# A fused window attention and expert mixture: one scaling step on ScalarE, an earlier landing time in the planner, and a new order of the work

## The chip, the cores and the metric

The kernel runs on 1 core of one Trainium2 chip. The metric is the device time of one execution in microseconds, as the median of the runs. The core's engines are TensorE (matmuls, PE in the profile; PEld is its weight load), VectorE (DVE), ScalarE (ACT), GpSimd (POOL) and SyncE (SP). Each has its own queue of instructions and works through it in order; PSUM has eight banks, and matmuls write there.

## The reference

Inputs are q, k, v of shape (4, 8, 768, 64), gate probabilities of shape (3072, 4), w1 of shape (4, 512, 1024) and w2 of shape (4, 1024, 512).

```python
scores = (q @ k.T) / sqrt(64)
keep = (pos_k < 4) | ((0 <= pos_q - pos_k) & (pos_q - pos_k < 128))
a = softmax(where(keep, scores, -1e9))
x = (a @ v).transpose(0, 2, 1, 3).reshape(3072, 512)
p = domain_probs / (domain_probs.sum(-1) + 1e-9)
out = sum over e of p[:, e] * (relu(x @ w1[e]) @ w2[e])
```

Attention sees a window of 128 keys and four sink keys; the mixture runs all four experts for every token.

## The kernel before, in words

**Tiles and groups.** Each of the four batches b has 768 tokens, cut into three groups g of 256; a pair (b, g) is the unit in which tokens pass from attention to the experts. Attention works on head pairs hp. For each (b, hp, g) it makes scores (L708, for the sinks L669), an exponential on ScalarE (L733), a mask product on VectorE (L727, L742), values (L767, L774), a reciprocal (L801) and a scaling (L804, L819). The result is turned into xT, with TensorE (L838) in batch 0 and with a transposing DMA (L791) after that.

**Experts.** Groups (0, 0) and (0, 1) are the *early* groups. For them the hidden rows H = relu(x w1) are made ungated. `emit_second` then multiplies by w2 in eight 512-column matmuls (L1579) for each half group s and expert e, into one of two `acc` banks. VectorE adds the result, scaled by the gate column, to `osbw`: L1589 writes the first (e = 0), L1591 adds the others. All other groups multiply the gate into H, sum all experts in PSUM, and use a scheme with seven block products in place of eight for the second matmul (L1493, names P1 to P7, in the order of CHAIN). VectorE prepares weight forms for it (L360 to L366) and sums of H blocks, S (L1434, L1411).

The first matmul also has a seven-product way (START says from which group for each expert), with its weight forms (L393 to L399) and token forms T (L1174): L1208 with 128 columns, or L1320 with 512 columns for the *turned units*. These last are the units of batches 2 and 3 but for the first four. They write H rows by token (L1341, L1345 and others), and a transposing DMA from SP (L1301) turns these into H. Units that don't take that way use L1118. A unit of the seven-product way takes two PSUM banks X and Y from a ring of six at P1, and one, V, at P5.

**What sets the order.** The Python program is a planner that writes a fixed order for each engine. It keeps a clock for each (`t`, with the costs in `pe`, `act`, `dve`, `pool`, `lands` and `sp`) and at every turn it lists what could go next on TensorE with a ready time and a priority (the lower number goes first): an attention step (DUE when it is due, 3 otherwise), a step of an open unit (2, plus STEP0 for each place in the list), a newly opened unit (OPEN when one is open already), a second product (1, or LOW_SECOND), or a block product (HIGH_PRODUCT when VectorE is BEHIND or many H tiles are live, LOW_PRODUCT otherwise). Attention is due by SHARE_OF, and a batch's attention begins by LEAD. OVER says by how many steps attention must be late before a single head pair's scores go without a partner. MIX bounds the early units left when later ones may open, FULL and NH (6) the live H tiles.

Work for VectorE and ScalarE goes into a list by `later(engine, ready, slack, run)`, and `flush` takes from it, of what is ready, what has the earliest `ready + slack`. The slacks are named: MASK for the mask product, GATE and GATE0 for the gated evictions, TOKEN for T, FORM for the weight forms, SCALED for ScalarE's second step on a turned row. MARGIN goes into the due time of S sums, and CHORES bounds how many of them stand in the list. SOON is the time from which weight forms are made. All these only set the order in the queues; semaphores do the real waiting.

**H rows.** In `emit_turning`, the DMA's time to land is counted by the same clock, and S sums and products of a unit are offered from then on:

```python
done = sp(at, issue=1330, takes=1400, turning=True) + LANDS
self.H_part[b, g, e](done)
```

where `sp` adds the issue, 800 ns, `takes` and 900 ns. EXPERTS gives the order of the four experts of a pair (all in order where it names none).

Of the kernel before, what the change touches and what calls it, by code (L numbers as in the profile page):

```python
# [9 lines left out]
ALU = mybir.AluOpType  # L10
# [6 lines left out]
def kernel(  # L17
# [12 lines left out]
    nc = tc.nc  # L30
# [5 lines left out]
    Ntok, Dout = out.shape  # L36
# [24 lines left out]
    TURN_ABOUT = 1  # L61
    OWN = 2
    TURNED_UNITS = (4, 0)
    EXPERTS = {(1, 0): (0, 2, 1, 3), (1, 1): (3, 2, 1, 0), (1, 2): (3, 2, 1, 0), (2, 2): (2, 0, 3, 1), (3, 1): (3, 2, 1, 0)}
    FIRST = 1
    START = {0: (1, 0), 1: (0, 2), 2: (0, 0), 3: (1, 0)}
    MIX = 6
    SHARE_OF = (1.01, 0.92, 0.96)
    LEAD = (1.01, 0.99)
    DUE = 1.9  # L70
    LOW_PRODUCT = 2.9
    LOW_SECOND = 2.7
    HIGH_PRODUCT = 1.9
    EARLY = -0.01
    MASK = 5000
    GATE = 800
    GATE0 = 300
    FORM = 6000
    TOKEN = 3000
    MARGIN = 500  # L80
    HOLD = 0
    FULL = 7
    STEP0 = 0.03
    READY = 40
    REST = 3000
    LANDS = 0
    SCALED = 300
    SHARED = 2
    MARGIN1, MARGIN2 = 4000, 14000
    OWNED_READ = 152  # L90
    WIDE = 2
    OPEN = 2.5
    SOON = 34000
    NEARLY = 2
    ROWED = 24000
    GATED = 38000
# [5 lines left out]
    MORE = 2  # L102
    BOTH = 1
    PAIR = 0
    OVER = 4
    ALONE = 2.0
    BEHIND = 1500
    CHORES = 3
    BIASED = 1
    FAST = tuple(START)  # L110
    BZ = 0
# [17 lines left out]
    def act(cols, *deps):  # L129
        at = max([t["act"], *deps])  # L130
        t["act"] = at + max(196, 68 + cols / 1.23)
        return at + max(350, 205 + cols / 1.2)
# [29 lines left out]
    def later(engine, ready, slack, run):  # L162

        pend.append((ready, ready + slack, engine, run))
# [255 lines left out]
    def next_form():  # L420
# [11 lines left out]
        forming.append(x)  # L432
        later("dve", t["pe"], FORM, run)
        return True
# [58 lines left out]
    for h in range(H):  # L493
        r = 32 * (h // 2) + NSINK * (h % 2)
        nc.sync.dma_start(
            out=vsf[r:r + NSINK, :, 0:D], in_=v[:, h, 0:NSINK, :].rearrange("b j d -> j b d"),
# [4 lines left out]
    for sgn in (1, -1):  # L501
        nc.gpsimd.affine_select(
            out=identf, in_=identf, compare_op=ALU.is_ge, fill=0.0,
# [6 lines left out]
    for tb in (2, 3):  # L510
# [21 lines left out]
        out=low[0].rearrange("p (n q) -> p n q", n=3)[:, 0::2], in0=two, scalar1=LOW, scalar2=-LOW, op0=ALU.mult, op1=ALU.add,  # L532
# [4 lines left out]
        out=sel2, in_=ident.rearrange("p (n c) -> p n c", c=32)[:, :, 0:2 * NSINK].rearrange("p n (a j) -> p n a j", a=2), axis=AX.X,  # L537
# [151 lines left out]
    def scores(b, hp, g, more=False):  # L689
# [34 lines left out]
        else:  # L724
            def mask_both(at):
                def run(engine):
                    nc.vector.tensor_mul(a, a, m[:, None, :].to_broadcast([P, 2, w]))  # L727
                    masked(dve(2 * w, rate=1.92))
                later("dve", at, MASK, run)
            part = join(2, mask_both)  # L730
# [226 lines left out]
    acc_free = [0.0, 0.0]  # L957
    out_sb = {}

    class Mixture:  # L960


        def __init__(self):
# [3 lines left out]
            for b, g in PAIRS:  # L967
                fast = [e for e in EXPERTS.get((b, g), range(E)) if self.is_fast(b, g, e)]
                slow = [e for e in range(E) if e not in fast]
# [40 lines left out]
        def halves(self):  # L1010
            return sum(x[0] <= t["pe"] + REST for x in self.resting)

# [52 lines left out]
        def firsts(self):  # L1065
# [4 lines left out]
            for i, u in enumerate(self.open):  # L1070
                b, g, e = u["unit"]
                if u["fast"]:
                    for m in u["left"]:
                        yield max(u["at"].get(m, 1e12), free_at() if m == "P5" else 0.0), 2 + STEP0 * i, (u, m)
                else:
                    j = u["left"][0]
                    yield self.unit_ready(b, g, e, j), 2 + STEP0 * i, (u, j)
            if n < WIDE and early:
                at, g = self.next_early()
                yield at, (OPEN if n else 2), ("early", g)  # L1080
            if n < WIDE and self.units and (self.units[0][0] or loaded) and early <= MIX and self.room() and not (early + zero and self.live >= NH - 1):
                yield self.unit_ready(*self.units[0], QF), (OPEN if n else 2) - EARLY, ("unit",)

        def emit_first(self, what, ready):
# [56 lines left out]
            def run(engine):  # L1141
# [5 lines left out]
                part(at)  # L1147
            later("dve", end, GATE0, run)

        def tokens(self):  # L1150
# [22 lines left out]
            def run(engine):  # L1173
# [4 lines left out]
                else:  # L1178
                    self.T_at[b, g] = done
            later("dve", at, TOKEN, run)  # L1180

        def emit_fast(self, u, m, ready):
# [67 lines left out]
            if m == "P1":  # L1250
                u["last"] = join(2, lambda at: gated(H[:, 1, :, 1], tiles["X"], 1, at, GATE, slots["X"]))

# [19 lines left out]
            elif m == "P2":  # L1272
                gated(H[:, 0, :, 1], y, 1, end, GATE, slots["Y"])
            elif m == "P7":
# [5 lines left out]
            elif m == "P3":  # L1280
                gated(H[:, 0, :, 0], y, 0, end, GATE, slots["V"])
            else:
                u["last"](end)

        def emit_turning(self, u, m, ready):
# [4 lines left out]
            if m in ("P1", "P5"):  # L1290
                spare = [i for i in range(6) if ring[i] <= ready + 40]
                spare.sort(key=lambda i: (whole[i], ring[i]))
                if m == "P1":
# [5 lines left out]
                    def turned(k):  # L1299
                        def turn(at):  # L1300
                            nc.sync.dma_start(  # L1301
                                out=H[:, k].rearrange("c f t n -> c (f t) n"), in_=X[k].rearrange("p f t n -> p (f t n)"), transpose=True,
                            )
                            done = sp(at, issue=1330, takes=1400, turning=True) + LANDS
                            self.H_part[b, g, e](done)
# [27 lines left out]
            def gated(k, s, src, ready, slack, slot=None, then=None):  # L1333
                gate = own_gates[:, 2 * ((b - OWN) * NG + g) + s, e:e + 1]

                def run(engine):
                    if engine == "act":
                        nc.scalar.activation(out=src, in_=src, func=AF.Relu)  # L1338

                        def scaled(engine):  # L1340
                            nc.scalar.mul(X[k][:, :, s], src, gate)  # L1341
                            done(act(n))
                        later("act", act(n), SCALED, scaled)
                        return
# [11 lines left out]
            if m == "P1":  # L1356
                u["last"] = join(2, lambda at: gated(1, 1, tiles["X"], at, GATE, slots["X"]))

# [19 lines left out]
            elif m == "P2":  # L1378
                gated(0, 1, y, end, GATE, slots["Y"])
            elif m == "P7":  # L1380
# [5 lines left out]
            elif m == "P3":  # L1386
                gated(0, 0, y, end, GATE, slots["V"])
            else:
# [54 lines left out]
        def until(self, b, g, e, m):  # L1443
            n = self.products.index((b, g, m)) * E + self.order_of(b, g).index(e) - self.piece
            return max(0.0, n * QF * G / 2.4 - MARGIN)

# [119 lines left out]
        def emit_second(self):  # L1566
            ready = self.second_ready()
            g, s, e = self.second.pop(0)
            if g not in out_sb:
                out_sb[g] = mo.tile([P, 2, Dout], FP32, name="osbw", tag=f"wide{g}", bufs=1)  # L1570
                if g == 0:
                    gates()
            dst = out_sb[g][:, s]
            bank = self.turn % 2
            self.turn += 1
            op = acc[bank]
            H = self.H[0, g, e]
            for fb in range(NFB):
                nc.tensor.matmul(  # L1579
                    op, lhsT=H[:, fb // QF, fb % QF, s], rhs=w2_sb[e][:, fb, :],  # L1580
                    start=(fb == 0), stop=(fb == NFB - 1),
                )
            end = pe(NFB * Dout, ready, n=NFB)
            acc_free[bank] = 1e12
            sc = scale_t[:, 2 * g + s, e:e + 1]

            def run(engine):
                if e == 0:
                    nc.vector.tensor_scalar(out=dst, in0=op, scalar1=sc, scalar2=None, op0=ALU.mult)  # L1589
                else:  # L1590
                    nc.vector.scalar_tensor_tensor(  # L1591
                        out=dst, in0=op, scalar=sc, in1=dst, op0=ALU.mult, op1=ALU.add,
                    )
                acc_free[bank] = at = dve(Dout, fixed=218)
                if e == E - 1:
                    r = (2 * g + s) * P
                    nc.sync.dma_start(out=out[r:r + P, :], in_=dst)
                    self.stored.append(sp(at))
            later("dve", end, 400, run)
            self.since = 0  # L1600
            self.done += NFB * Dout
            if s == 1:
                self.live -= 1
                left[e] -= 1
                if not left[e]:
                    used.add(e)
# [55 lines left out]
    while mix.more() or att.more():  # L1662
# [46 lines left out]
        mix.chore()  # L1709
        if ahead or now > SOON:  # L1710
            next_form()
        if ahead + 1 < B and not att.more() and (ahead == 0 or (ahead + 1, 0) in turned_at) and (ahead == 0 or mix.done >= sum(work[:ahead]) * LEAD[ahead - 1]):
            ahead += 1
# [5 lines left out]
            upto = mix.done  # L1719
        share = (sum(work[:ahead]) - upto) * SHARE_OF[max(ahead - 1, 0)]  # L1720
        due = ahead == 0 or att.steps * share <= (mix.done - upto) * att.total
        opts = []
        if att.more():
            late = ahead == 0 or (att.steps + OVER) * share <= (mix.done - upto) * att.total
            for r, step in att.options():
                p = (DUE if due else 3) - 0.1 * (step == "two")
                if step == "one" and not late:
                    p = max(p, DUE + ALONE)
                opts.append((max(r, now), p, "att", step))
        s2, p = mix.second_ready(), mix.product_ready()  # L1730
        behind = max(t["dve"] - now, 0.0) + 500 * sum(x[2] == "dve" and x[0] < now + 300 for x in pend)
        opts.append((max(p, now), HIGH_PRODUCT if behind > BEHIND or mix.live >= FULL or wide and TURN_ABOUT and mix.turn_about else LOW_PRODUCT, "product", None))
        joins = due and ahead >= PAIR and att.two() and not late and len(mix.open) >= HOLDS
        opts += [(max(f, now), p, "first", x) for f, p, x in mix.firsts() if not (joins and x[0] in ("unit", "early"))]
        opts.append((max(s2, now), 1 if mix.since >= 1 else LOW_SECOND, "second", None))
        soonest = min(o[0] for o in opts)
# [61 lines left out]
```

## Time and profile before

| | us |
|---|---|
| median of 3 runs (353.9 to 354.16) | 354.09 |
| span of the profiled execution | 351.9 |
| TensorE busy | 346.2 |
| VectorE busy | 282.8 |
| ScalarE busy | 208.3 |
| GpSimd busy | 71.6 |

The profiled execution's own time is given by its span, from the first to the last instruction; the device time of the runs is 2.2 us longer than that, which lies around the span. The granted TensorE clock is 1.000 over the span. TensorE's busy time counts matmuls that overlap and whose ends are modelled, so it is read together with the starts of the matmuls. In the windows view a line has the window, its length, and for PE, PEld, DVE, ACT and POOL the busy us and the number of instructions, then the granted clock, the DMA engines' use and GB/s. In a line of the timeline the first two columns are start and duration; what stands in brackets is idle time of the engine and what ended it.

### The profile page before, as it was taken

The numbers are of one execution on the slowest core, as the hardware profiler recorded it, in microseconds if no ns is written. First come the engines' busy times: TensorE is split into PE (matmuls) and PEld (weight loads), VectorE is DVE, ScalarE is ACT, GpSimd is POOL, SyncE is SP. The second block draws the span as 40 slices with busy tenths as digits, with TensorE's granted clock in tenths as the row PEclk, the third lists the DMA queues.
The fourth block names the chain that finished last, engine by engine and source line by source line (L and its number), as shares of the span: only waits on it lengthen the run. The fifth ranks groups of instructions, "written<-read, shape, count | busy, mean of one in ns | idle before, by whom it ended". The sixth has DMA issues, their size and how long they took to land.

```text
span 351.9 us, 9351 instructions
## 1 busy us (share of the span) xinstructions
PE 346.2 (98%) x3721; PEld 266.0 (76%) x3721; DVE 282.8 (80%) x672; ACT 208.3 (59%) x476; POOL 71.6 (20%) x89
## 2 busy tenths in 40 slices
PE   8999999999999999999999999999999999999996
PEld 3685769656789998998999886755856676666685
DVE  5886999878999999799898999578768586675740
ACT  6863624447874443647453539689589767666611
POOL 8946114330546206100152000000000000000000
PEclk9999999999999999999999999999999999999999
DMA  9999999999999999920999602545437733545441
GB/s 178 178 188 195 223 214 181 179 160 174 162 147 165 121 145 122 132 64 9 109 173 159 113 32 62 120 101 120 80 91 174 127 89 93 120 120 115 67 120 61
DMA packets 161032, 45.61 MB, mean 130 GB/s; under 512 B 144740, under 2 KB 156996, under 8 KB 160988
## 3 DMA queue, kind: packets, MB, share of 16 engines
q0 software_dynamic: 79104, 17.31, 56.4%
q1 hardware_dynamic: 80828, 27.18, 40.1%
q8 instruction: 29, 0.48, 0.5%
q10 hardware_dynamic: 1056, 0.52, 0.5%
q14 instruction: 15, 0.12, 0.1%
HBM read 38.39 MB, written 6.34 MB: 127 GB/s over the span
## 4 chain that ended last, share of the span: by engine, by line
PE 75%; DMA 19%; POOL 5%; issue 1%; ACT 0%; POOLq 0%; SPq 0%
PE acc L1493 35%; PE cps L1320 17%; PE cps L1208 15%; DMA w<-in_moe_w_dram 12%; DMA qkn<-in_k_dram 4%; DMA qkT<-qkn 3%; PE sps L708 3%; PE od L774 2%; POOL qkn L251 2%; POOL w L331 1%; POOL vx L318 1%; PE hps L1118 1%; PE od L767 1%; POOL w L341 0%; PE acc L1579 0%
## 5 line engine op out<-in xcount | busy, mean ns | idle before, releaser
L1493 PEld LDWEIGHTS <-H 128*128 128x128 bf16 x708 | 66.5, 98 | 17.9 <-issue 1.1
L1493 PE MATMUL acc<-w,H 128*128 128x256 bf16 x420 | 56.9, 273 | 0.0
L733 ACT ACTIVATE aT<-sps 128x512 bf16<-128x512 f32 (+1 forms) x96 | 47.2, 579 | 16.3 <-PE sps L708 16.2
L1208 PEld LDWEIGHTS <-w 128*128 128x128 bf16 x640 | 39.1, 98 | 1.2 <-issue 0.5
L1493 PEld LDWEIGHTS <-S 128*128 128x128 bf16 x320 | 30.3, 98 | 9.5 <-issue 0.8
L1241 DVE SCALAR_TENSOR_TENSOR H<-cps,gates 128x512 bf16<-128x512 f32 x54 | 36.6, 683 | 0.0
L1338 ACT ACTIVATE cps<-cps 128x512 f32<-128x512 f32 x44 | 25.5, 585 | 17.5 <-PE cps L1320 17.0
L1118 PE MATMUL hps<-xT,w 128*128 128x256 bf16 x256 | 31.9, 273 | 0.1
L819 ACT ACTIVATE onat<-od,R 128x64 bf16<-128x64 f32 x108 | 24.9, 324 | 11.4 <-DVE R L801 11.1
L318 POOL DMA_DIRECT2D vx<-in_v_dram x24 | 21.4, 903 | 43.0 <-PE od L774 31.2
L1208 PEld LDWEIGHTS <-vf 128*128 128x128 bf16 x480 | 29.3, 98 | 1.0 <-issue 0.5
L1579 PE MATMUL acc<-w,H 128*128 128x512 bf16 x128 | 29.9, 379 | 0.0
L1493 PE MATMUL acc<-wf,H 128*128 128x256 bf16 (+1 forms) x216 | 29.6, 272 | 0.0
L1118 PEld LDWEIGHTS <-w 128*128 128x128 bf16 x256 | 24.1, 98 | 4.7 <-issue 0.9
L1341 ACT ACTIVATE rest<-cps,own_gates 128x512 bf16<-128x512 f32 x37 | 25.5, 693 | 0.7
L727 DVE TENSOR_TENSOR aT<-aT,mask 128x1024 bf16<-128x1024 bf16 (+1 forms) x36 | 22.7, 640 | 3.1 <-ACT aT L733 2.8
L251 POOL DMA_DIRECT2D qkn<-in_q_dram x22 | 19.7, 896 | 23.3 <-DMA qkT<-qkn 14.7
L1208 PE MATMUL cps<-T,w 128*128 128x128 bf16 x320 | 24.3, 219 | 0.0
L1208 PE MATMUL cps<-xT,w 128*128 128x128 bf16 x320 | 24.1, 219 | 0.0
L1320 PE MATMUL cps<-w,T 128*128 128x512 bf16 x80 | 23.8, 379 | 0.0
L1320 PE MATMUL cps<-vf,T 128*128 128x512 bf16 x80 | 23.6, 379 | 0.0
L1554 ACT COPY osb<-acc 128x256 f32<-128x256 f32 x32 | 12.1, 382 | 19.3 <-PE acc L1493 19.1
(145 smaller groups left out, 673.5 us busy)
## 6 DMA issues: line engine op xcount, KB each, us to landing
w<-in_moe_w_dram POOLq DMA_DIRECT2D x6, 1024.0 KB, 18.4
out_dram<-osb SPq DMA_DIRECT2D x16, 256.0 KB
vx<-in_v_dram POOLq DMA_DIRECT2D x24, 128.0 KB, 6.5
qkn<-in_q_dram POOLq DMA_DIRECT2D x22, 128.0 KB, 6.7
qkn<-in_k_dram POOLq DMA_DIRECT2D x22, 128.0 KB, 7.4
gates<-gate_rows SPq DMA_DIRECT2D x20, 128.0 KB
w<-in_moe_w_dram POOLq DMA_DIRECT2D x4, 256.0 KB, 6.9
w<-in_moe_w_dram POOLq DMA_DIRECT2D x2, 512.0 KB, 11.5
```

Of the source, the lines that this page charges most:

```text
L251: nc.gpsimd.dma_start(out=both[:, i], in_=src[b, :, tb * P:(tb + 1) * P, :].rearrange("h p d -> p h d"),)
L318: nc.gpsimd.dma_start(out=vx[tb][:, :, 0:D], in_=v[b, :, tb * P:(tb + 1) * P, :].rearrange("h p d -> p h d"),)
L733: nc.scalar.activation(out=a[:, ph], in_=sps[ph][:, 0:w], func=AF.Exp, scale=scale)
L819: nc.scalar.mul(o[:, qi, hp, ph * D:(ph + 1) * D], od[:, qi, ph, 0:D], R[:, qi, ph])
L1118: nc.tensor.matmul(h[:, i].rearrange("p (q n) -> p q n", q=2), lhsT=w1_sb[e][:, db, fb * P:(fb + 1) * P], rhs=xT[b, g][:, :, db], start=(i ...
L1208: nc.tensor.matmul(y[:, f], lhsT=A[:, d, f * P:(f + 1) * P], rhs=T[:, d], start=(m in ("P1", "P5") and f == 0 and d == 0), stop=(d == 1), ...
L1241: nc.vector.scalar_tensor_tensor(out=dst, in0=src, scalar=0.0, in1=gate, op0=ALU.max, op1=ALU.mult)
L1320: nc.tensor.matmul(y.rearrange("p f n -> p (f n)"), lhsT=T[:, d], rhs=A[:, d], start=(m in ("P1", "P5") and d == 0), stop=(d == 1), skip_g ...
L1338: nc.scalar.activation(out=src, in_=src, func=AF.Relu)
L1341: nc.scalar.mul(X[k][:, :, s], src, gate)
L1493: nc.tensor.matmul(y, lhsT=self.operand(b, g, e, m)[:, f], rhs=forms[e][m][:, f, cs], start=(k == 0 and f == 0 and m in (("P1", "P5", "P2" ...
L1579: nc.tensor.matmul(op, lhsT=H[:, fb // QF, fb % QF, s], rhs=w2_sb[e][:, fb, :], start=(fb == 0), stop=(fb == NFB - 1),)
```

## The change

The first scaled product of each early group and half (e = 0) is written by ScalarE, with `nc.scalar.mul` by the gate column, and is put into ScalarE's list; the `acc` bank is counted free by ScalarE's cost. LANDS goes from 0 to -1400, so turned H rows are counted as ready 1.4 us sooner by the planner's clock. The planner's other numbers and the order of the experts are set anew; this changes the order of instructions on all engines.

```diff
-    EXPERTS = {(1, 0): (0, 2, 1, 3), (1, 1): (3, 2, 1, 0), (1, 2): (3, 2, 1, 0), (2, 2): (2, 0, 3, 1), (3, 1): (3, 2, 1, 0)}
+    EXPERTS = {(1, 0): (2, 0, 3, 1), (1, 1): (0, 2, 1, 3), (1, 2): (0, 3, 1, 2), (2, 2): (1, 2, 3, 0), (3, 1): (1, 3, 0, 2), (3, 2): (2, 0, 1, 3), (2, 0): (3, 1, 2, 0), (0, 2): (3, 0, 2, 1), (3, 0): (2, 1, 0, 3), (2, 1): (0, 1, 2, 3), (0, 1): (0, 1, 3, 2)}
-    MIX = 6
-    SHARE_OF = (1.01, 0.92, 0.96)
-    LEAD = (1.01, 0.99)
-    DUE = 1.9
+    MIX = 9
+    SHARE_OF = (1.08, 0.91, 0.91)
+    LEAD = (0.98, 1.025)
+    DUE = 1.2
-    LOW_SECOND = 2.7
-    HIGH_PRODUCT = 1.9
-    EARLY = -0.01
-    MASK = 5000
-    GATE = 800
-    GATE0 = 300
-    FORM = 6000
-    TOKEN = 3000
-    MARGIN = 500
+    LOW_SECOND = 2.9
+    HIGH_PRODUCT = 1.3
+    EARLY = -0.1
+    MASK = 12000
+    GATE = 1300
+    GATE0 = 1500
+    FORM = 13000
+    TOKEN = 4000
+    MARGIN = 0
-    FULL = 7
-    STEP0 = 0.03
+    FULL = 8
+    STEP0 = 0.16
-    REST = 3000
-    LANDS = 0
-    SCALED = 300
+    REST = 3500
+    LANDS = -1400
+    SCALED = 100
-    OPEN = 2.5
-    SOON = 34000
+    OPEN = 1.8
+    SOON = 24000
-    OVER = 4
-    ALONE = 2.0
-    BEHIND = 1500
-    CHORES = 3
+    OVER = 7
+    ALONE = 1.8
+    BEHIND = 2200
+    CHORES = 6
...
             def run(engine):
                 if e == 0:
-                    nc.vector.tensor_scalar(out=dst, in0=op, scalar1=sc, scalar2=None, op0=ALU.mult)
-                else:
-                    nc.vector.scalar_tensor_tensor(
-                        out=dst, in0=op, scalar=sc, in1=dst, op0=ALU.mult, op1=ALU.add,
-                    )
+                    nc.scalar.mul(dst, op, sc)
+                    acc_free[bank] = act(Dout)
+                    return
+                nc.vector.scalar_tensor_tensor(
+                    out=dst, in0=op, scalar=sc, in1=dst, op0=ALU.mult, op1=ALU.add,
+                )
                 acc_free[bank] = at = dve(Dout, fixed=218)
...
-            later("dve", end, 400, run)
+            later("dve" if e else "act", end, 400, run)
```

## The prediction

> **What bounds the kernel now.** First the page's busy line, the windows by stage and the list of waits of TensorE (columns: engine, line, what it waited for; us in total, times, longest).
>
> ```profile
> PE 346.2 (98%) x3721; PEld 266.0 (76%) x3721; DVE 282.8 (80%) x672; ACT 208.3 (59%) x476; POOL 71.6 (20%) x89
> ```
> ```profile
> 40.00:60.00 20.00, 20.00 (x211) 15.47 (x209) 19.08 (x36) 6.45 (x14) 5.01 (x6) 1.00 1.47 205
> 90.00:120.00 30.00, 30.00 (x419) 26.38 (x417) 29.78 (x79) 19.64 (x60) 16.00 (x19) 1.00 1.75 143
> 240.00:270.00 30.00, 30.00 (x260) 19.90 (x258) 23.26 (x55) 23.50 (x49) 0.00 (x0) 1.00 0.45 105
> ```
> ```profile
> PE acc L584 <- DVE lent L489: 1.4, 1, 1.4
> PE sinks L669 <- DMA qkT<-qkn: 0.3, 1, 0.3
> PE tx L838 <- DVE onat L804: 0.2, 1, 0.2
> ```
>
> TensorE is busy all through, at the full granted clock (the 1.00 near the end of each window line), and waits for almost nothing. VectorE is its equal in one stage only, 90 to 120 us: 29.78 of 30. But matmuls overlap, and busy time can hide short waits. So I go by starts: the chain of waits, in order of time, has stretches of unbroken matmuls (start, us, what).
>
> ```profile
> 87.17 1.73 PE acc L1579 x8
> 103.44 2.62 PE acc L1493 x24
> 119.19 3.57 PE cps L1208 x64
> 228.34 3.03 PE cps L1320 x14
> ```
>
> One 512-column matmul takes 1.73 / 8 = 0.216 us, one of 256 columns 2.62 / 24 = 0.109, one of 128 columns 3.57 / 64 = 0.0558. From the first expert matmul (15.58 us) to the end of the last (348.72) is 333.1 us. Counts by shape give: 1104 L1493 and 256 L1118 at 0.109 = 148.2; 128 L1579 and 280 L1320 at 0.2155 = 87.9; 1120 L1208 at 0.0558 = 62.5; 32 short L1493 = 1.8. Attention beside them, from starts in the timeline: 328 L774 at 0.029 = 9.5, 64 L767 at 0.0555 = 3.6, 34 transposes 1.9, 26 visits to the score matmuls 15.2. In all 330.6. **TensorE loses at most 2.5 us after 15.58.** I can point at 1.5 of it; the largest pieces are in the timeline of TensorE (start, us, what):
>
> ```profile
> 20.24 0.28 PE L774 MATMUL od<-vx,aT 128*128 128x65 bf16 x4
> 20.61 0.28 PE L838 MATMUL tx<-ident,onat 128*128 128x128 bf16 x2
> ...
> 84.24 1.46 PE L1579 MATMUL acc<-w,H 128*128 128x512 bf16 x6
> 85.99 0.29 PE L669 MATMUL sinks<-qkT,ksd 128*32 128x256 bf16 x4 [0.30 <-DMA qkT<-qkn]
> ```
>
> Four L774 at 0.029 would end at 20.36: 0.25 lost. Six L1579 end at 85.54: 0.46 lost. The rest are 0.22 at 22.3, 0.14 at 79.4, 0.11 at 102.5, 0.10 at 140.2, 0.15 at 242.4 and 0.08 at 17.3.
>
> **What cannot move.** The number of matmuls is the same: START, which says which experts take the seven-product way, and the number of turned units are unchanged. Before 15.58 only attention and fillers are on offer and only their mutual order counts; DUE goes from 1.9 to 1.2, below 2 both times. After the last matmul 3.2 us of copy and store stay. MIX has no effect once two early units have been opened, which has happened when group (0,2) is first allowed; FULL 7 or 8 is never reached with six H tiles; EXPERTS for (0,1) and (0,2) is not read. Only one kind of matmul can come or go: the one that marks bank Y of a unit when the bank last held a narrow tile. Before has none; each would be 0.215 us, and I take 0, with +0.9 (four of them) as the bound. So the sum is over 333 us of TensorE alone.
>
> **First scaled product on ScalarE.** The rows by line: L1589 (VectorE, x4, 27.6 to 33.4 us) has a median of 752 ns; the nearest ScalarE row is the scaled one.
>
> ```profile
> L1341 ACT ACTIVATE rest<-cps,own_gates 128x512 bf16<-128x512 f32 x37 | 25.5, 693 | 0.7
> L1338 ACT ACTIVATE cps<-cps 128x512 f32<-128x512 f32 x44 | 25.5, 585 | 17.5 <-PE cps L1320 17.0
> ```
>
> L1341 has the same scaling by a column, L1338 the same f32 output; 585 to 693, and I take 693. VectorE loses 4 x 0.75 = 3.0 us, ScalarE gains 2.8. Nobody waited for L1589 and VectorE itself idled 2.7 us before it, waiting for TensorE, so on the path it is worth 0. Bounds: four evictions each 0.06 sooner give -0.2; one behind a 0.6 us exponential with TensorE at the bank gives +0.6. What hides it: two acc banks, each filled for 1.73 us, and ScalarE at 11.3 of 20 us. The next reader of the same rows comes at 42.9 us.
>
> **Turned rows counted sooner (LANDS 0 to -1400).** No instruction changes; on its clock the kernel counts 1330 + 800 + 1400 + 900 = 4430 ns from issue to landing, and now 3030. The trace has one place where the landing ends a wait: SP's timeline and VectorE's.
>
> ```profile
> 333.89 2.58 SPq L1301 DMA_TRANSPOSE H<-rest x2
> ```
> ```profile
> 338.12 0.42 DVE L1434 TENSOR_TENSOR S<-H 128x512 bf16<-128x512 bf16 x1 [2.76 <-DMA H<-rest]
> ```
>
> The second of two issues starts 1.24 after the first, at about 335.2; it is used at 338.1: 2.9 us. So 3030 is nearer than 4430 and is still not short. Value 0: from 205 us on TensorE has only the 0.15 at 242.4 to get back. Bounds: -0.2, and +1.0 where the queue is loaded (rival D).
>
> **The refitted order.** Two things can be had. (a) The waits: 1.5 seen, 2.5 at most, none at least. Nearly all end at an attention step set a little before its data were there. Now SHARE_OF and LEAD move the attention of the later batches and OPEN 1.8 keeps a second unit open, so that more steps are ready beside it; I take half of 1.5, -0.8. (b) Visits to the score matmuls, from starts:
>
> ```profile
> 91.83 0.40 PE L708 MATMUL sps<-qkT 64*128 64x128 bf16 x6
> 92.15 0.61 PE L1493 MATMUL acc<-w,H 128*128 128x256 bf16 x4
> ...
> 94.59 0.62 PE L708 MATMUL sps<-qkT 64*128 64x128 bf16 x12
> 95.14 0.61 PE L1493 MATMUL acc<-w,H 128*128 128x256 bf16 x4
> ```
>
> A single head holds TensorE for 0.32, a pair for 0.55, and the matmul ahead of either takes 0.205 rather than 0.109. A pair saves 2 x (0.33 + 0.10) - (0.55 + 0.10) = 0.21. Six singles stand between 86 and 101 us and two after 219; OVER from 4 to 7 lets a single go ahead only when attention is further behind. At most four pairs, -0.8; at least 0; I take two, -0.4. The looser deadlines (MASK, GATE, GATE0, FORM, TOKEN) only change who goes first on VectorE; I cost them at 0 because six PSUM banks and the products lie between. Without that cover they are rival C.
>
> Sum: span 351.9, plus 2.2 around it (median 354.09 less the span), less 0.8 and 0.4: **352.9 us**. With every term at its best, 354.1 - 2.5 - 0.8 - 0.4 = 350.4.
>
> The row that I trust for TensorE's room is the spacing of starts: 2.5 us. The Trainium skill's Perfetto Trace Analysis, "Identifying the Most-Contended Engine", says that matmul occupancy misjudges the distance to roofline and that the busy share of weight loads is to be used; that is 76% here. By that rule some 84 us would be open, and an order alone could bring the time below 350. This trace does not agree: in 240 to 270 loads are busy 19.9 of 30 while a 512-column matmul (0.215) covers a load of 0.098.
>
> **Rivals.**
>
> B, no change: what one stage regains another loses, as the same TensorE sum is only dealt anew. 354.0 (353.4 to 354.8). For it: 1.2 us is all that I found. Against: so many costs reset rarely cancel. 0.20.
>
> C, slower: VectorE becomes the bound from 90 to 210 us. A seven-product unit costs it four gated evictions at 0.685 and two sums at 0.69, 4.1 us, against 56 x 0.0558 = 3.1 on TensorE; its products cost VectorE four sums at 0.42 and a fifth of an us more, 1.9, against 28 x 0.109 = 3.05. Together 6.0 against 6.2, and 0.22 us of idle in 90 to 120. Each unit run ahead of its products puts VectorE 1.0 behind. GATE0 (300 to 1500), CHORES (3 to 6) and OPEN let three sums of 1.26 stand before an eviction that frees a bank. It decides once VectorE is over two units behind, when all six banks are held; two or three units past that cost 2 to 3 us: 356.6. Against it: BEHIND still turns to products. 0.20. The Trainium skill's Perfetto Trace Analysis says in the same section that occupancy is a fair measure for VectorE; by that rule 90 to 120 is its roofline already, and the 29.78 of 30 agrees.
>
> D, slower: rows counted landed that are not. Forming S then blocks VectorE, as for 2.76 us at 335. Transposes queued behind stores land up to 1.3 late; three such, with half hidden, +2, less 0.8 for what the refit wins: 355.3. 0.10.
>
> E, more room than the sum of starts: below 350.4, as by the weight-load rule. Spacing speaks against it. 0.02.
>
> **How the numbers follow.** The forecast holds 0.48: mostly 351.4 to 353.4. About 0.2% (0.7 us) is what a measurement of this kernel can tell from no change. Faster is the forecast and E, 0.50; same is B, 0.20; slower C and D, 0.30. The forecast's own range is 351.2 to 353.4; to hold 8 in 10 the range takes in B, D and the lower half of C: 351.2 to 356.6.
>
> **What would show it.** Right: still some 3721 matmuls and TensorE from 15.6 us at under 332 us; fewer than 26 score visits; four 0.6 to 0.7 us rows on ScalarE near 30 us; the 0.25 and 0.46 gone. C: VectorE full past 120 us, TensorE waits behind L1241 or L1261. D: VectorE's waits for DMA H above 2.8 us in sum. I am wrong if the matmul count changes, if the stretch before 15.6 changes, or if the gaps found do not account for the difference.

## The result, and the profile after

The kernel after takes 354.74 us (median of 7 runs, 354.46 to 355.3), the kernel before 353.9 in the same session; the ratio is 1.0024, interval 1.0014 to 1.0035. It is slower, by 0.84 us. The forecast was 352.9.

The page's busy line, three windows and TensorE's list of waits, as shown of before:

```profile
PE 346.0 (98%) x3698; PEld 266.7 (76%) x3721; DVE 283.0 (80%) x670; ACT 208.6 (59%) x481; POOL 72.3 (20%) x89
```
```profile
40.00:60.00 20.00, 19.89 (x211) 15.44 (x212) 18.09 (x36) 6.35 (x13) 4.79 (x6) 1.00 1.48 203
90.00:120.00 30.00, 30.00 (x438) 27.21 (x436) 29.49 (x72) 19.15 (x55) 10.29 (x12) 1.00 1.10 119
240.00:270.00 30.00, 29.61 (x259) 20.47 (x262) 23.43 (x58) 23.34 (x58) 0.00 (x0) 1.00 0.47 115
```
```profile
PE acc L584 <- DVE lent L489: 1.4, 1, 1.4
PE sps L708 <- ACT onat L819: 0.2, 1, 0.2
PE acc L1579 <- issue: 0.2, 1, 0.2
PE tx L838 <- DVE onat L804: 0.2, 1, 0.2
```

The busy line hides the change. The 3721 weight loads are all there, but 23 matmul records are missing; each leaves a hole of 0.216 us, the length of one 512-column matmul, in these windows too, and is no wait (the 0.2 "issue" before L1579 is such a hole). So again I go by starts. **From the first expert matmul to the end of the last, TensorE takes 333.84 us; it was 333.13 in the profile of before, and 332.78 in a second profile of the same kernel (e1).** The longer of these two has 0.36 at 86 us that the other lacks. What is new in the kernel after, in its timeline:

```profile
35.50 0.45 PE L708 MATMUL sps<-qkT 64*128 64x128 bf16 x6
36.06 1.03 PE L1118 MATMUL hps<-xT,w 128*128 128x256 bf16 x8
...
136.49 0.61 PE L1493 MATMUL acc<-w,S 128*128 128x256 bf16 x4
137.16 0.61 PE L1208 MATMUL cps<-T,w 128*128 128x128 bf16 x8
...
241.36 0.71 PE L1493 MATMUL acc<-w,H 128*128 128x256 bf16 x5
242.25 0.40 PE L708 MATMUL sps<-qkT 64*128 64x128 bf16 x6 [0.18 <-ACT onat L819]
...
283.29 0.60 PE L1493 MATMUL acc<-qkn,H 128*128 128x256 bf16 x4
284.00 0.38 PE L1320 MATMUL cps<-w,T 128*128 128x512 bf16 x1
```

Six score matmuls alone took 0.33 in before; here 36.06 - 35.50 = 0.56, so 0.23 is a wait. Four L1493 take 0.44: 137.16 - 136.49 loses 0.23, and 284.00 - 283.29 loses 0.27. Five of them and the step into a score visit take 0.64: at 242.25 TensorE loses 0.25. In the same way 0.21 inside the score visit at 244, 0.12 at 236, 0.08 at 263.5 and 0.06 twice (120 and 163 us): 1.5 us of new waits. Gone are 0.14 at 79.4, 0.12 at 102.5, 0.10 at 140.2 and 0.15 at 242.4. The difference, 1.0, is nearly all of the 1.06 us between 333.84 and 332.78.

Two of the old places, for comparison with the lines shown of before:

```profile
20.67 0.28 PE L774 MATMUL od<-vx,aT 128*128 128x65 bf16 x4
21.04 0.29 PE L838 MATMUL tx<-ident,onat 128*128 128x128 bf16 x2
...
84.28 1.67 PE L1579 MATMUL acc<-w,H 128*128 128x512 bf16 x7
85.90 0.29 PE L669 MATMUL sinks<-qkT,ksd 128*32 128x256 bf16 x4
```

The 0.25 after the values is still there. At 86 us nothing is lost now: seven L1579 and the step into the visit end at 85.90. That step takes 0.10 here, with no wait; so of the 0.46 that the prediction counts there, 0.36 was a wait.

The moved write, by line (duration min/median/max in ns), and VectorE's waits for a transposed H:

```profile
L1589 ACT ACTIVATE osbw<-acc,scale_t x4: 687/688/690, 27.8 to 33.9; 128x512 f32<-128x512 f32 x4
```
```profile
DVE S L1434 <- DMA qkT<-rest: 1.6, 1, 1.6
DVE S L1434 <- DMA H<-rest: 0.2, 1, 0.2
```

ScalarE takes 688 ns for each (I had taken 693). Waits for landings are 1.8 in sum, 2.8 before: nothing here shows rows that were counted as landed too soon.

### The profile page after: what moved, and what is told of

The parts are those of the page before. It is cut to its first block, busy times and chain, and to the rows that moved or that the text cites. A ratio compares the mean times of both kernels' runs of the same rounds, so it can differ in the third digit from the quotient of the medians.

```text
span 353.0 us, 9317 instructions
## 1 busy us (share of the span) xinstructions
PE 346.0 (98%) x3698; PEld 266.7 (76%) x3721; DVE 283.0 (80%) x670; ACT 208.6 (59%) x481; POOL 72.3 (20%) x89
## 4 chain that ended last, share of the span: by engine, by line
PE 89%; ACT 4%; DVE 3%; issue 2%; DMA 1%; ACTq 0%
PE acc L1493 33%; PE cps L1208 18%; PE cps L1320 14%; PE acc L1579 8%; PE hps L1118 7%; PE sps L708 3%; PE od L774 2%; PE acc L584 2%; ACT aT L733 1%; PE od L767 1%; DMA H<-rest 1%; DVE onat L804 1%; PE tx L838 1%; ACT cps L1338 1%; DVE aT L742 0%
## 5 line engine op out<-in xcount | busy, mean ns | idle before, releaser
L1493 PEld LDWEIGHTS <-H 128*128 128x128 bf16 x708 | 66.7, 98 | 18.6 <-issue 1.1
L1493 PE MATMUL acc<-w,H 128*128 128x256 bf16 x420 | 56.3, 273 | 0.2
L1493 PEld LDWEIGHTS <-S 128*128 128x128 bf16 x320 | 30.5, 98 | 9.1 <-issue 0.6
L1241 DVE SCALAR_TENSOR_TENSOR H<-cps,gates 128x512 bf16<-128x512 f32 x54 | 36.4, 686 | 0.0
L819 ACT ACTIVATE onat<-od,R 128x64 bf16<-128x64 f32 x116 | 27.0, 325 | 12.9 <-DVE R L801 12.6
L1338 ACT ACTIVATE cps<-cps 128x512 f32<-128x512 f32 x41 | 23.8, 587 | 14.9 <-PE cps L1320 14.2
L1493 PE MATMUL acc<-wf,H 128*128 128x256 bf16 (+1 forms) x216 | 30.2, 271 | 0.1
L1579 PE MATMUL acc<-w,H 128*128 128x512 bf16 x121 | 29.2, 379 | 0.5 <-issue 0.2
L1208 PE MATMUL cps<-T,vf 128*128 128x128 bf16 x320 | 22.9, 219 | 0.0
L1320 PE MATMUL cps<-vf,T 128*128 128x512 bf16 x78 | 22.7, 379 | 0.2
L1320 PE MATMUL cps<-w,T 128*128 128x512 bf16 x75 | 22.4, 379 | 0.2
```

Source lines behind the costliest of these rows:

```text
L819: nc.scalar.mul(o[:, qi, hp, ph * D:(ph + 1) * D], od[:, qi, ph, 0:D], R[:, qi, ph])
L1208: nc.tensor.matmul(y[:, f], lhsT=A[:, d, f * P:(f + 1) * P], rhs=T[:, d], start=(m in ("P1", "P5") and f == 0 and d == 0), stop=(d == 1), ...
L1241: nc.vector.scalar_tensor_tensor(out=dst, in0=src, scalar=0.0, in1=gate, op0=ALU.max, op1=ALU.mult)
L1320: nc.tensor.matmul(y.rearrange("p f n -> p (f n)"), lhsT=T[:, d], rhs=A[:, d], start=(m in ("P1", "P5") and d == 0), stop=(d == 1), skip_g ...
L1493: nc.tensor.matmul(y, lhsT=self.operand(b, g, e, m)[:, f], rhs=forms[e][m][:, f, cs], start=(k == 0 and f == 0 and m in (("P1", "P5", "P2" ...
L1579: nc.tensor.matmul(op, lhsT=H[:, fb // QF, fb % QF, s], rhs=w2_sb[e][:, fb, :], start=(fb == 0), stop=(fb == NFB - 1),)
```

## The experiments

**My first theory**: the order owns the loss, ScalarE's write and LANDS are free. The rivals: one of these two owns it. Stretch is from the first expert matmul to the end of the last, by starts; visits are the score visits in it. Ratios are to the kernel before, run on the same chip.

| run | median us | ratio, interval | first expert matmul at | stretch us | visits |
|---|---|---|---|---|---|
| e1 before, unchanged | 353.80 | 1.0003, 0.9994 to 1.0011 | 16.50 | 332.78 | 26 |
| e2 before, write on ScalarE, order kept | 353.92 | 1.0005, 0.9996 to 1.0014 | 16.03 | 333.00 | 26 |
| e3 before, LANDS | 353.95 | 1.0006, 0.9997 to 1.0015 | 15.67 | 333.30 | 26 |
| e4 the other numbers alone | 356.63 | 1.0080, 1.0066 to 1.0094 | 15.78 | 335.72 | 30 |
| after | 354.74 | 1.0024, 1.0014 to 1.0035 | 16.02 | 333.84 | 27 |
| e5 after, write on VectorE, order kept | 354.90 | 1.0033, 1.0020 to 1.0046 | 15.59 | 334.51 | 27 |
| e6 after, CHORES, MARGIN of before | 355.53 | 1.0047, 1.0033 to 1.0060 | 16.29 | 334.81 | 30 |
| e7 after, attention numbers of before | 357.09 | 1.0095, 1.0082 to 1.0109 | 16.45 | 336.16 | 28 |
| e8 after, unit numbers of before | 354.82 | 1.0031, 1.0020 to 1.0043 | 16.10 | 333.80 | 26 |
| e9 after, sums first | 355.16 | 1.0043, 1.0029 to 1.0058 | 15.71 | 334.44 | 27 |
| e10 before, sums first | 356.48 | 1.0075, 1.0063 to 1.0088 | 16.39 | 335.46 | 26 |
| e11 as e9, one write back | 355.52 | 1.0044, 1.0029 to 1.0059 | 16.38 | 334.25 | 27 |
| e12 e3 with sums first | 356.07 | 1.0060, 1.0048 to 1.0073 | 16.03 | 335.20 | 26 |
| f1 e3, sums first late | 353.76 | 0.9998, 0.9990 to 1.0007 | 15.88 | 332.74 | 26 |
| f2 after, sums first late, one write back | 354.56 | 1.0021, 1.0012 to 1.0030 | 15.89 | 333.35 | 27 |
| f3 before, deadlines of after | 356.67 | 1.0081, 1.0068 to 1.0095 | 16.44 | 335.75 | 32 |
| f4 before, attention numbers of after | 356.02 | 1.0068, 1.0056 to 1.0081 | 15.87 | 335.26 | 29 |
| g1 after, LANDS 0 | 355.84 | 1.0058, 1.0044 to 1.0072 | 15.92 | 335.01 | 28 |
| g2 after, no write on ScalarE | 355.89 | 1.0069, 1.0056 to 1.0082 | 16.34 | 335.50 | 29 |

### Each part alone

e1: no edit.

> The kernel before, unchanged. Every theory expects a ratio of 1.000 within 0.001. The profile tells how much the first expert matmul (15.59 us before, 16.02 after) moves between executions of one program: if by chance alone, its start differs from 15.59 by up to 0.5 us here too, and with it the span.

The start of the first expert matmul moves by 0.9 us between two executions of one program. In e1 it comes late and the wait of 0.36 at 86 us is gone: the DMA that ended it landed at 85.86 in the profile of before and at 85.89 in e1, and TensorE came to it only at 86.53. Over all profiles but that of e7 this landing lies between 85.4 and 86.2, and the wait is in 5 of them (before, e3, e6, e12 and f1). Time that TensorE gains ahead of 86 can be given back there.

e2: the order of TensorE, GpSimd and SP stays as it is.

```diff
-                    nc.vector.tensor_scalar(out=dst, in0=op, scalar1=sc, scalar2=None, op0=ALU.mult)
+                    nc.scalar.mul(dst, op, sc)
```

> The kernel before with only the engine of the four first scaled products changed to ScalarE; the planner's clock still charges VectorE, so the order on TensorE, GpSimd and SP is the same. Theory (the order owns the loss): 1.000, within 0.1%. Rival (the write on ScalarE itself costs, behind other ScalarE work while TensorE needs the bank): +0.3 to +0.8 us, 1.001 to 1.002, with waits of TensorE near 27 to 34 us.

No difference by time. The trace has a cost: the 0.23 at 35.5 us is in it, which neither trace of before has. The fourth write stands on ScalarE ahead of the exponentials that free the banks of the scores, as ScalarE's timeline in e2 shows:

```profile
33.87 0.69 ACT L1589 ACTIVATE osbw<-acc,scale_t 128x512 f32<-128x512 f32 x1 [0.48 <-PE acc L1579]
34.45 2.05 ACT L733 ACTIVATE aT<-sps 128x512 bf16<-128x512 f32 x4
```

e3, then e4:

```diff
-    LANDS = 0
+    LANDS = -1400
```

> The kernel before with only LANDS at -1400. Theory (the order owns the loss, and each new deal of the order moves the time by some tenths of a us either way): 0.998 to 1.002. Rival (rows counted landed too early): slower by the whole 0.8 us, 1.0024, with VectorE's waits for DMA H longer than 2.8 us in sum.

No difference by time. In the trace the 0.15 at 242 went and 0.27 at 307 came; VectorE's one wait for H is 3.0 us, 2.8 in e1.

```diff
 # the kernel after, with
-    LANDS = -1400
+    LANDS = 0
-                    nc.scalar.mul(dst, op, sc)
+                    nc.vector.tensor_scalar(out=dst, in0=op, scalar1=sc, scalar2=None, op0=ALU.mult)
```

> The kernel after with the first scaled products back on VectorE and LANDS back at 0, so that only the other numbers and the expert order differ from before. Theory: the loss is here, 1.002 to 1.004. Rivals: 1.000 if the loss belongs to ScalarE's write or to the landing time.

The loss is in the numbers and the expert order, as the theory had it, but it is 2.9 us and not 0.84. So the parts don't add up: what is nothing in the order of before is worth 2 us under the new numbers. My first theory was half right. Of the 2.94 us by which e4's stretch is longer than e1's, some 2.0 are waits, 0.74 of them in front of L1579 at 29.8. The rest goes with four more score visits and with one more matmul, of 0.216, at 82.4: it is the one that marks bank Y, which the prediction took as 0. It stays away in the kernel after, but comes once in e4, e8, f3 and g2 and three times in e7.

### What the two small parts are worth under the new numbers

e5 moves the write back, with the order of TensorE kept; g2 also moves the planner's charge, g1 takes LANDS away.

```diff
 # e5, in the kernel after
-                    nc.scalar.mul(dst, op, sc)
+                    nc.vector.tensor_scalar(out=dst, in0=op, scalar1=sc, scalar2=None, op0=ALU.mult)
                     acc_free[bank] = act(Dout)
```

> The kernel after with only the engine of the four first scaled products put back to VectorE; the planner still charges ScalarE, so the order on TensorE is that of the kernel after. Theory: the new numbers make weight forms from 24 us on and fill VectorE there, so ScalarE's write covers a wait: TensorE loses about 0.7 us near 30 us, in front of L1579, and the ratio to before rises from 1.0024 to about 1.0045. Rival (the move is free in both orders, as in e2): 1.0024.

TensorE's and VectorE's timelines in e5:

```profile
27.81 1.24 PE L1579 MATMUL acc<-w,H 128*128 128x512 bf16 x5
29.77 1.89 PE L1579 MATMUL acc<-w,H 128*128 128x512 bf16 x8 [0.72 <-DVE osbw L1589]
```
```profile
28.36 0.69 DVE L395 TENSOR_TENSOR vf<-vf,w 128x1024 bf16<-128x1024 bf16 x1
28.97 0.75 DVE L1589 TENSOR_SCALAR osbw<-acc,scale_t 128x512 f32<-128x512 f32 x1
```

Five L1579 would end at 28.89; the next comes at 29.77, so 0.88 is lost in front of L1579: the new numbers put two weight forms (L393, then the L395 shown) ahead of the first write, where before has none. SOON 24000, which lets forms be made from 24 us on, would do that; no run changes SOON alone. The 0.23 at 35.5 is gone in exchange: 0.88 - 0.23 = 0.65 is nearly all of the 0.67 by which the stretch grows (334.51 - 333.84). The theory of a cover is shown in the trace but not by time: the median moves by 0.16 only, and the interval of e5 holds 1.0024 as well as 1.0045.

> The kernel after with LANDS back at 0: the order on TensorE is the same up to the turned units. If LANDS pays back most of the 2 us: about 1.006. If ScalarE's write does: 1.003 or less.

> The kernel after with the first scaled products on VectorE and charged there, LANDS at -1400. If ScalarE's write pays back most of the 2 us, 0.7 directly (e5) and the rest by the order that was fitted with it: about 1.007. If LANDS does: 1.0045, as e5.

Against the kernel before on the same chip, g1 is 2.2 us slower, g2 2.25, e4 2.9 and the kernel after 0.84. So leaving out either part costs 1.4, and leaving out both 2.1, not 2.8. Neither owns the 2 us. My reading is that the numbers hold for the planner's clock that has both, and that with either missing the order is dealt anew; no run separates that from chance.

### Is there one owner among the numbers?

e6, e7 and e8 put groups back in the kernel after; f3 and f4 put groups of after into the kernel before.

```diff
 # e6: CHORES, MARGIN of before
 # e7: SHARE_OF, LEAD, DUE, OVER, ALONE of before
 # e8: OPEN, EARLY, STEP0, LOW_SECOND, HIGH_PRODUCT of before
 # f3, in before: MASK, GATE, GATE0, FORM, TOKEN, SCALED, MARGIN, CHORES, BEHIND of after
 # f4, in before: SHARE_OF, LEAD, DUE, OVER, ALONE of after
```

> The kernel after with CHORES back at 3 and MARGIN at 500, so that fewer S sums stand in VectorE's list. Theory (S sums ahead of the sums L1261 and L1367 own the waits of 0.22 at 137 and 0.27 at 284 us): these two go, 1.0005 to 1.0015. Rival (any new deal of the order moves waits about, and the loss has no single owner): anything from 1.000 to 1.006, with waits at other places.

> The kernel after with SHARE_OF, LEAD, DUE, OVER and ALONE of before: attention is set by the old times among the new rest. If attention's place owns the loss (waits of score matmuls at 242 and 244, one at 35.5): 1.000 to 1.001. If the numbers fit only each other: slower than after, 1.003 to 1.008, with more score visits.

> The kernel after with OPEN, EARLY, STEP0, LOW_SECOND and HIGH_PRODUCT of before: units are opened by the old priorities. If keeping a second unit open owns the loss: 0.999 to 1.001. If the numbers fit only each other: 1.003 to 1.008.

> The kernel before with MASK, GATE, GATE0, FORM, TOKEN, SCALED, MARGIN, CHORES and BEHIND of after. If the looser deadlines own the loss (rival C of the prediction): 1.003 to 1.008, with VectorE's idle time lower and waits of TensorE from 90 to 210 us. If the loss has no single owner: also slower than before, since each number is fitted to the rest, but not by all of 2.9 us; 1.001 to 1.004.

> The kernel before with SHARE_OF, LEAD, DUE, OVER and ALONE of after. If attention's place owns the loss: 1.003 to 1.008 with waits of score and value matmuls. If no single owner: 1.001 to 1.004. Fewer than 26 score visits after 15.6 us if OVER works as the prediction had it; 26 or more if not.

Among these groups, no: none that goes back wins anything. Against the kernel before, e6 is 1.9 us slower and e7 3.4, where the kernel after is 0.84 slower; e8 can't be told from after by time, and has its stretch. Going forward by a group costs 2.3 to 3.0. The waits are at other places: in f3 0.74 at 283 for ScalarE's L1360, in f4 0.60 at 126 for the sum L1261 and 0.60 at 273. In e6 the 0.27 at 284, which was to go, stays. f3 costs as much as all numbers together (3.0, e4 2.9) and f4 nearly as much (2.3), which I had not expected. Score visits rose to 32 and 29. Not one of these orders has the 24 visits that I counted on. The expert order (EXPERTS), SOON, REST, MIX and FULL are in none of these groups, so an owner among them is not ruled out.

### Taking single waits away with the order kept

e9 holds back S sums by one place, where the sum that P7 and P3 need stands next; the queues of the other engines stay as they are.

```diff
+    held_sums = []
 # S sums (L1434, L1411) go to held_sums, and are issued before any other
 # VectorE instruction, product or new unit, but after this one:
                     def run(engine):
                         nc.vector.tensor_add(tiles["V"], c5, tiles["X"])
                         at["P7"] = at["P3"] = dve(n)
+                        release()
```

> The kernel after; TensorE, ScalarE, GpSimd and SP keep their order. On VectorE alone, in five places where S sums (L1434, L1411) stood directly ahead of the sum L1261 or L1367 that a unit's P7 and P3 wait for, that sum goes first. Theory (these S sums own the waits at 137 and 284 us): the two go, 0.4 to 0.5 us less than after, 1.001 relative to before. Rival (the waits come from ScalarE or from TensorE's own order): as after, 1.0024.

The waits at 137 and 284 went, so S sums did cause them. But the stretch rose by 0.6, at another place (in e9 lines are shifted: L1507 is L1493, L1447 is L1434):

```profile
102.59 1.04 PE L1507 MATMUL acc<-wf,S 128*128 128x256 bf16 x8
104.02 0.61 PE L1507 MATMUL acc<-wf,S 128*128 128x256 bf16 x4 [0.40 <-DVE S L1447]
```

Eight end at 103.46, so 0.56 is lost: in the stage where VectorE is full, the sums held back were themselves due. Up to 117 us 0.34 more follows.

> The kernel before with the same rule on VectorE: the sum that P7 and P3 wait for goes ahead of S sums that stood directly before it; all other queues keep their order. Before has one wait of 0.15 that is of a unit (242.4), and there the sum already followed its last input. Theory: 1.000, within 0.1%. Rival (S sums ahead of sums cost before too): 0.999.

> As e9, and the last of the four first scaled products is back on VectorE, where it stands ahead of no weight form; the other three stay on ScalarE. Theory (on ScalarE it holds up the exponential of the next scores, and TensorE 0.23 us at 35.5): 0.23 us less than e9, 1.0004 relative to before. Rival (0.23 is no cost, since TensorE waits for a DMA at 86 in any case): as e9.

> The kernel before with LANDS at -1400 (e3) and the rule of e9 on VectorE. e3 had lost the wait of 0.15 at 242 and had a new one of 0.27 at 307, where S sums stood ahead of L1367. Theory: that one goes, 0.3 us less than e3 and 0.9995 relative to before. Rival: as e3, 1.0005.

e10 and e12 lose 0.9 at 111 in the same way, and 1.0 more at 140, where scores wait for the gated eviction L1241, which stands behind three sums of L1411; the rule is wrong from 90 to 140. In e12 the 0.27 at 307 is gone. e11 takes the 0.23 at 35.5 away (stretch 0.19 less than e9), which the median doesn't show. So the rule was kept for turned units alone:

> The kernel before with LANDS at -1400, and on VectorE the sum L1367 ahead of S sums for turned units only (after 205 us). e12 showed from 240 us on 0.05 us of waits, against 0.31 in e3 and 0.24 in the kernel before. Theory: 0.25 us less than e3, ratio 0.9995 to 1.0000. Rival (the swap costs here too): 1.002 or more.

> The kernel after with the same swap for turned units only, and the last of the four first scaled products on VectorE. Theory (waits add up): 0.27 at 284 and 0.23 at 35.5 go, 0.5 us less than after, ratio 1.001. Rival: 1.0024, as the time is given back at the next step that waits.

In f2 TensorE's timeline and VectorE's (L1328 is L1320, L1375 is L1367, L1445 is L1434, L1505 is L1493):

```profile
282.94 0.60 PE L1505 MATMUL acc<-qkn,H 128*128 128x256 bf16 x4
283.38 0.38 PE L1328 MATMUL cps<-w,T 128*128 128x512 bf16 x1
```
```profile
282.44 0.69 DVE L1375 TENSOR_TENSOR cps<-rest,cps 128x512 f32<-128x512 f32 x1
283.04 0.42 DVE L1445 TENSOR_TENSOR S<-S,H 128x512 bf16<-128x512 bf16 x1
```

Four products in 0.44 and no wait. In the kernel after, whose timeline is 0.35 later here, an S sum came first, and L1320 started at 284.00:

```profile
282.91 0.42 DVE L1434 TENSOR_TENSOR S<-S,H 128x512 bf16<-128x512 bf16 x1
283.26 0.69 DVE L1367 TENSOR_TENSOR cps<-rest,cps 128x512 f32<-128x512 f32 x1
```

The stretch is 333.35, 0.49 less than after, as 0.27 and 0.23 say. The ratios differ by 0.0003, 0.1 us, and 1.001 lies just outside the interval, so of the expected 0.5 the time shows a part at most. f1 is the best that I found and equals the kernel before (353.76 to 353.70); no run beats the kernel before.

## Why the prediction was wrong, point by point

**The bound** was right: TensorE is full from 15.6 us on, the same 3721 weight loads are there, and the waits account for nearly all of the difference. (Its sum of shapes counts 34 transposes; the trace has 32 after 15.58, which changes 0.1.) A changed stretch before 15.6, which the prediction took for a sign of being wrong, is none: it changes by 0.9 us in e1, with nothing edited.

**The step that failed is (a) of the refitted order.** I counted 1.5 us of waits, took half as won, and put the cost of new waits at nothing within the forecast. Some old waits did go: 0.14, 0.12, 0.10, 0.15, and the 0.36 at 86. New ones of 1.5 came. And the 0.36 can't be put down to the order: it ends with a DMA, and comes and goes between two profiles of one program (before and e1). Those at 17, 20 and 22 us (0.55) are in all 20 profiles. What this order had to win was some 0.5 us, not 1.5, and against that stand the 1.5 that the forecast put at nothing. Of the new waits, 0.73 have a cause that an experiment took away with TensorE's order kept: ScalarE's fourth write (0.23, e11 and f2) and S sums (0.23 at 137 in e9, 0.27 at 284 in e9 and f2).

**Step (b)** had the wrong sign: 27 visits, not 24. OVER at 7 did not join heads in any run that has it; f4 has 29, but changes SHARE_OF, LEAD, DUE and ALONE too, so OVER alone stays untested.

**The start of the sum** was off by 0.2. I set 2.2 us around the span; in the runs it is 1.7 (354.75 against 353.0), so the profiled execution of before was one of about 353.6. But the sum starts in effect from the median of three runs, 354.09, and that of seven is 353.9.

**ScalarE's write** at 0 was right for the old order by time (e2, 0.23 in the trace), wrong for the new one: there it saves 0.67 of the stretch (e5). I had named the cover of TensorE's wait, but not that weight forms would fill VectorE just there. **LANDS** at 0 was right alone (e3); rival D did not come.

**Rival C** had its mechanism in part: S sums ahead of a sum that a unit waits for cost 0.23 + 0.27 (e9, f2). But VectorE was no fuller at 90 to 120 (29.49 against 29.78) and the price was 0.5, not 2 to 3. VectorE need not be two units behind for such a wait: one S sum is enough. **Rival B** was near in kind, and its range (to 354.8) holds 354.74: the sum was dealt anew, gains and losses both came, and the losses were larger.

**The weight-load rule** (rival E) would have left 84 us, an estimate from the 24% of the span in which loads are not busy. The Trainium skill's Perfetto Trace Analysis, "Identifying the Most-Contended Engine", takes the busy share of weight loads, next to the share of peak FLOP/s (MFU), for TensorE's distance to roofline. That busy share is 76% in both kernels, while the edits here moved the time by up to 3.4 us upwards (e7) and in no run measurably down; the spacing of starts read this kernel, the share did not.

What stays open: the waits at 242 and 244 (0.46) and at 236. The trace names ScalarE's L819 for the first, which would be a bank held by a value tile; no run with TensorE's order kept took it away. Why f3 and f4 cost about as much as all numbers together isn't explained beyond their waits, visits and the one matmul more in f3.

## What to carry to other kernels

Where one engine is full and starts leave 1 to 2 us in 333, a new order of this planner should be priced as a draw whose new waits are as large as the old ones: the eighteen edited kernels here came out +0.06 to +3.4 us from the old one. Numbers of a planner that are set together couldn't be priced one by one here, and a small edit that is free in one order may be what another order stands on. Compare by the spacing of starts between two fixed matmuls, profile the unchanged kernel twice, and count a wait that a DMA ends as won only if it is in both of these profiles.

## What the runs showed of the hardware

The first expert matmul starts between 15.59 and 16.50 us in the 19 profiles of after and of these runs, whose instructions up to there are the same for TensorE. The difference lies in when the first matmuls double their rate. Matmuls of 512 columns start 0.427 us apart at first and 0.216 later, those of 256 columns 0.213 and 0.109, those of 128 columns 0.107 and 0.056. In the profile of before the rate doubles some 2.9 us after the first matmul, in the one of after some 4.6 us, and in e1, the same program as before, not until some 5.8 us. The granted clock that the profile shows is 1.00 in these stretches too. This moves the first expert matmul by up to 0.9 us, as much as the effect that was looked for (0.84); of e1's 0.9 the span shows 0.5, since the wait of 0.36 at 86 us went. The runs of one kernel on one chip spread by 0.35 to 1.05 us.

The transposing DMA that the sink scores (L669) near 86 us wait for was issued at about 75 us and landed between 85.4 and 86.2 in all profiles but that of e7. The move from full-array matmuls into a visit of 64-row score matmuls costs 0.096 us (0.205 between starts in place of 0.109).
